# One-core attention and gated-MLP kernel: late key tiles of the last block by 256 queries, and a written-out order in place of the scheduler

## The chip, the cores and the metric

The kernel runs on one core of one Trainium2 chip. Five engines of that core take part: TensorE (matrix products, PE in the profile, its weight loads as PEld), VectorE (DVE), ScalarE (ACT), GpSimd (POOL) and SyncE (SP), which issues the transfers. The metric is device time in microseconds for one launch, the median of the runs of one kernel. A profile shows one execution and tells times from the span's start.

## What is computed

Layer norm of `x` (2048 x 512), then attention with 32 heads of 16 columns and a gated MLP of width 1792, both on the normalised input, both added to `x`:

```python
xn = _layernorm(x)
qkv = (xn @ wqkv).reshape(B, S, 3, H, Dh)            # S 2048, H 32, Dh 16
scores = einsum("bhqd,bhkd->bhqk", q, k) * Dh ** -0.5
o = einsum("bhqk,bhkd->bhqd", softmax(scores), v)
gate = xn @ W_gate;  up = xn @ W_up
return x + o.reshape(B, S, D) @ wo + (relu(gate) * up) @ W_down
```

All inputs and the output are bfloat16.

## The kernel before

**Blocks and units.** Attention runs in 32 blocks `(c4, gg, ee)`: four chunks of 512 queries, four groups of eight heads, and in each the even or the odd four heads. A block goes over 16 key tiles of 128 keys. The exponentials of one key tile (four heads by 512 queries) are made in one of two ways. As two *units*: TensorE writes scores of two heads by 512 queries into one of two pairs of PSUM banks (two operations, one on each half of the partitions), and ScalarE takes the exponential of all 128 x 1024 in one instruction into a ring of 16 buffers (L1546). Or as a *quad*: four score tiles go through one PSUM bank each to VectorE, which turns them into 16-bit integers that read as bfloat16 approximate the exponential (L1502), and two shifted patterns are added by GpSimd (L1516, for the first two and last two quads by VectorE). `QUADS` says how many of a block's 16 tiles are quads; over all blocks these are 160 of 512 tiles, and 704 units are left.

**Weighted sums.** `pv_stream` multiplies the exponentials with the values, which carry a column of ones, so that the row sum of the softmax comes along. One operation is four weight loads and four matmuls of 32 output rows each, on one half of the partitions; the halves are two operations. A unit pair gives two operations, a quad six. They accumulate over the block in one PSUM bank; in the last block the two halves have a bank each (`LAST2`). `normalise` copies the bank to SBUF, sends the row sums through two small transfers (`rsum`, `rb<-rrec`), spreads the reciprocals (L1417) and multiplies (L1420).

**The end of the kernel.** For the last block, `normalise_last` works without transfers. ScalarE copies one bank (L1291), VectorE adds the other (L1293), transposes 32 x 32 blocks so that row sums stand where they can be read (L1296), takes reciprocals (L1297), transposes them back (L1298) and multiplies (L1300); first for queries 0 to 255 of the chunk, then for 256 to 511. Each half is followed by the product with the last rows of `wo`, for two tiles of 128 output rows (`stream_out`), and the sum with the residual that was put aside earlier (`resid`, L1319); row tile 3 gets its residual from TensorE by an identity matmul (L1275) and leaves through ScalarE (L1315, L1326). The products with the two earlier head groups, four operations for each row tile, are put on TensorE behind the last weighted sums.

**Filling.** Projections, the MLP and the output rows are cut into operations that are spread over the units as `jobs`; their weights come by transfers paced to units (`paced`; W_down by `load_wd`, one tile of 14 each `D_STEP` units).

**Order.** Every operation is an `Op` with its readers and writers. `Graph.run` gives them their order: a greedy list scheduler with modelled durations, latencies and slacks (`DMA_SLACK`, `REC_SLACK`, `MUL_SLACK`), which takes the operation that can start first and, among equals, the one of least `prio`. It also chooses the buffer of each pool, and puts blank matmuls into TensorE's gaps at the start. `emit` then writes each engine's queue in that order, with a semaphore wait only where an engine has not seen the event yet. Every engine works its queue in order.

Of the kernel before, what the change touches and what calls it, by code (L numbers as in the profile page):

```python
# [12 lines left out]
ALU = mybir.AluOpType  # L13
# [22 lines left out]
D_STEP = 3.5  # L36
# [18 lines left out]
TOGETHER = 0  # L55
LAST2 = 1
LASTD = 2
TAIL_ACT = (3,)
# [14 lines left out]
QUAD_SHIFT = {(1, 3): 1, (2, 1): -1, (4, 0): -1, (6, 0): 1, (6, 3): 1, (7, 0): 1, (7, 2): 1, (8, 1): 1, (8, 4): 1, (8, 5): 1, (9, 0): 1, (9, 3): -1, (13, 1): -1, (16, 0): -1, (16, 3): 1, (18, 4): -1, (20, 2): 1, (23, 0): -1, (25, 4): -1, (26, 2): -1, (28, 0): 1, (28, 3): -1, (29, 3): 1, (30, 0): -1, (31, 1): 1}  # L73
# [14 lines left out]
QUADS = [0, 2, 5, 5, 6, 6, 4, 5, 6, 5, 5, 5, 6, 5, 5, 8, 5, 5, 4, 6, 6, 4, 6, 5, 5, 5, 5, 5, 5, 6, 5, 5]  # L88
# [44 lines left out]
class Op:  # L133
    __slots__ = ("eng", "dur", "fn", "deps", "order", "prio", "acq", "name", "idx", "start", "end",
                 "done", "left", "users", "signal", "sem", "val", "waits", "stream", "lat", "seq", "cseq", "hb", "after", "mode", "half", "bank", "urgent", "slack", "port",
                 "load", "wsrc", "wkey", "wwaits", "pair", "held")
# [9 lines left out]
class Graph:  # L146
# [5 lines left out]
    SWITCH = 107.0  # L152
    TO_POOL = 110.0
    ISSUE = 16.0
    FILL = 425.0
    NEAR = 20
    OWN = 90.0
    DMA_SLACK = 1000
    FILL_MIN = 230.0
    AHEAD_LOADS = 4  # L160
    EARLY = True
    REUSE = 5
    WIRE_LAT, WIRE_KB = 1300.0, 6.1
    WARM_AT, COLD = 7300.0, 2.0

    def __init__(self):
        self.ops = []
        self.fillers, self.nfill, self.twins = [], 0, []
        self.units = {}
# [46 lines left out]
    def run(self):  # L216
        ops = self.ops
        for o in ops:
            o.users = []
            o.held = []  # L220
        for t in {t for o in ops for t in o.acq} | {c for o in ops for t in o.acq for c in t.pool.cur if c is not None}:
            us = set(t.w + t.r)
            t.left = len(us)
            for o in us:
                o.held.append(t)
        for o in ops:
            if o.after is not None and int(o.after) > 0:
                o.order.add(self.units[min(int(o.after), len(self.units)) - 1])
            pre = set(o.deps) | o.order
            o.left = len(pre)  # L230
            for d in pre:
                d.users.append(o)
        cand = {e: [] for e in self.ENGS}
        free = {e: 0.0 for e in self.ENGS}
        self.queue = {e: [] for e in self.ENGS}
        for o in ops:
            if o.left == 0:
                cand[o.eng].append(o)
        n = 0

        def slot_for(t):

            best, second = None, None
            for i in (t.allowed if t.allowed is not None else range(len(t.pool.cur))):
                c = t.pool.cur[i]
                if c is None:
                    at = 0.0
                else:
                    at = release.get(c)
                    if at is None:  # L250
                        if c.left:
                            continue
                        at = release[c] = max(u.end for u in c.w + c.r)
                if best is None or at < best[0]:
                    best, second = (at, i), best
                elif second is None or at < second[0]:
                    second = (at, i)
            if t.pool.shared:
                held = any(c is not None and c.open > 0 for c in t.pool.cur)
                if t.extra:  # L260
                    if t.extra.slot is None:
                        return None
                elif t.open:
                    if held and not (self.EARLY and second is not None):
                        return None
                elif len(t.allowed) > 3 and (not held or any(b.slot is None and b.extra.slot is not None for b in self.twins)):
                    return second
            return best


        pe = {"mode": "full", "at": -1e9, "free": [0.0, 0.0]}
        last = {}

        known, release = {}, {}

        def bound(o):
            at = 0.0
            for d in o.deps:
                at = max(at, (self.TO_POOL if o.eng == "POOL" and d.eng not in ("POOL", "SP") else 0.0) + d.end - (self.OWN if d.eng == o.eng == "DVE" else 0.0) if d.eng == "PE" or d.eng == o.eng == "DVE" else d.end + ((0.0 if d.urgent else max(self.DMA_SLACK, o.slack)) if d.eng == "SP" else o.slack))
            for d in o.order:  # L280
                at = max(at, d.start if d.eng == o.eng else d.end)
            return at

        def ready(o):
            at = known.get(o)
            if at is None:
                at = known[o] = bound(o)
            for t in o.acq:
                if t.slot is not None:
                    continue  # L290
                b = slot_for(t)
                if b is None:
                    return None
                at = max(at, b[0] + (o.slack if o.eng == "SP" else 0.0))
            return at
# [1306 lines left out]
```

## Time and profile before

| | us |
|---|---|
| runs | 678.15, 683.24, 683.33 |
| median | 683.24 |
| profiled execution | 683.3 |
| its span | 681.3 |
| exponentials, busy (704) | 651.9 |
| ScalarE busy in all | 659.9 |
| VectorE busy | 591.3 |
| GpSimd busy | 334.6 |

The granted clock of TensorE was 1.00 in the profiled execution, 0.98 in its last 6.3 us. In the page's rows an engine's line is followed by the instruction, what it writes and reads, how often it ran, busy time, mean of one in ns, and then the engine's idle time just before it with what ended that. A row of the timeline has start, length, engine and line, and in square brackets the idle time before it. "Issue" is a wait for nothing that the profile shows. The mean of a matmul (375 ns) is its modelled length in a pipeline, not the distance of two.

### The profile page before, as it was taken

Reading aid. Unit: us, or ns where it says so; the run is one execution under the profiler, and the core shown is the slowest. Engines: PE = TensorE matmul, PEld = TensorE weight load, DVE = VectorE, ACT = ScalarE, POOL = GpSimd, SP = SyncE. Lnnn points to the kernel's source line nnn. Section 1 sums busy time; section 2 is a strip of 40 time slices with the busy share of each in tenths; the row PEclk is TensorE's granted clock in tenths of the full one; section 3 lists DMA queues with packets and bytes.
Section 4 is the critical chain, followed back from the end, with each engine's and each line's share of the span. In section 5 each row is a group of like instructions: output and inputs, shape, how many; then the busy total and the mean of one; then the engine's idle time right before and its main releaser. Section 6 shows DMA issues by size and latency. Waiting matters only on the chain.

```text
span 681.3 us, 46196 instructions
## 1 busy us (share of the span) xinstructions
PE 669.6 (98%) x22355; PEld 410.7 (60%) x20975; DVE 591.3 (87%) x1001; ACT 659.9 (97%) x721; POOL 334.6 (49%) x345
## 2 busy tenths in 40 slices
PE   8999999999999999989999999999999999999997
PEld 3456576565575765656665665556565666666664
DVE  8948999998998887989999788899989877889886
ACT  7999999999999999999999999999999999999995
POOL 3301445554455554645555564655456644435640
PEclk9999999999999999999999999999999999999999
DMA  7511011132201021110101011011200122120001
GB/s 217 79 37 28 19 39 39 40 95 67 86 12 28 24 63 36 26 47 12 45 4 36 27 49 49 24 25 28 52 6 17 32 59 60 42 52 21 23 13 34
DMA packets 51479, 28.78 MB, mean 42 GB/s; under 512 B 18840, under 2 KB 50328, under 8 KB 51288
## 3 DMA queue, kind: packets, MB, share of 16 engines
q1 hardware_dynamic: 51144, 25.70, 14.7%
q8 instruction: 169, 2.77, 1.8%
q14 instruction: 22, 0.18, 0.1%
q10 hardware_dynamic: 144, 0.13, 0.1%
HBM read 18.22 MB, written 2.10 MB: 30 GB/s over the span
## 4 chain that ended last, share of the span: by engine, by line
PE 94%; DVE 4%; DMA 1%; issue 1%; POOL 0%; DVEq 0%; SPq 0%
PE ps L141 94%; DVE qd L1502 1%; DVE stats L831 1%; DMA rb<-rrec 1%; DMA x_sb<-in_A_x_dram 0%; DVE xn_sb L854 0%; DVE mv L833 0%; DVE up_sb L1151 0%; DVE xnT L899 0%; PE ps L1275 0%; DVE qT L1086 0%; DVE xn_sb L1319 0%; DVE hT L1155 0%; DVE kT L992 0%; DVEq L605 0%
## 5 line engine op out<-in xcount | busy, mean ns | idle before, releaser
L1546 ACT ACTIVATE ring<-ps 128x1024 bf16<-128x1024 f32 x704 | 651.9, 1063 | 9.6 <-PE ps L141 8.4
L141 PE MATMUL ps<-qT,kT 64*32 64x512 bf16 x8192 | 473.6, 375 | 3.6 <-DVE qd L1502 1.8
L1516 POOL INT64_ADD qd<-qd x312 | 321.8, 1042 | 305.7 <-DVE qd L1502 189.2
L1502 DVE TENSOR_SCALAR qd<-ps 128x512 int16<-128x512 f32 x640 | 418.8, 684 | 52.1 <-PE ps L141 46.9
L141 PE MATMUL ps<-qd,v_aug 64*32 64x512 bf16 x3840 | 306.7, 375 | 0.5 <-issue 0.2
L141 PE MATMUL ps<-ring,v_aug 64*32 64x512 bf16 x2816 | 245.3, 375 | 0.8 <-issue 0.7
L1482 PEld LDWEIGHTS <-kT 64*32 64x32 bf16 x8164 | 182.2, 92 | 105.7 <-issue 26.1
L1454 PEld LDWEIGHTS <-v_aug 64*32 64x32 bf16 x5304 | 132.6, 92 | 58.9 <-issue 7.4
L141 PE MATMUL ps<-xnT,wus 64*32 64x512 bf16 x1792 | 136.4, 375 | 0.0
L141 PE MATMUL ps<-xnT,wgs 64*32 64x512 bf16 x1792 | 136.0, 375 | 0.1
L141 PE MATMUL ps<-Wd,hT 64*32 64x512 bf16 x768 | 59.5, 375 | 0.2 <-issue 0.2
L934 PEld LDWEIGHTS <-hT 64*32 64x32 bf16 x1792 | 45.8, 92 | 22.2 <-issue 3.9
L934 PEld LDWEIGHTS <-wgs 64*32 64x32 bf16 x1792 | 44.4, 92 | 22.3 <-issue 4.4
L934 PEld LDWEIGHTS <-wus 64*32 64x32 bf16 x1792 | 45.1, 92 | 19.5 <-issue 3.0
L141 PE MATMUL ps<-Wk,hT 64*32 64x512 bf16 x512 | 43.0, 375 | 0.0
L1151 DVE COPY up_sb<-ps 128x512 f32<-128x512 f32 x56 | 38.3, 684 | 5.3 <-PE ps L141 5.1
L1155 DVE SCALAR_TENSOR_TENSOR hT<-ps,up_sb 128x512 bf16<-128x512 f32 x56 | 38.2, 682 | 3.6 <-PE ps L141 3.4
L141 PE MATMUL ps<-Wv,hT 64*32 64x512 bf16 x512 | 40.3, 376 | 0.2 <-issue 0.2
L141 PE MATMUL ps<-xnT,Wq 64*32 64x512 bf16 x480 | 39.3, 375 | 0.0
L141 PE MATMUL ps<-Wo_p,x_sb 64*32 64x512 bf16 x480 | 37.8, 376 | 0.0
L141 PE MATMUL ps<-xnT,Wk 64*32 64x512 bf16 x480 | 35.7, 375 | 0.3 <-DVE xnT L899 0.3
L141 PE MATMUL ps<-Wv,xnT 64*32 64x512 bf16 x512 | 33.0, 375 | 0.4 <-issue 0.2
(83 smaller groups left out, 221.9 us busy)
## 6 DMA issues: line engine op xcount, KB each, us to landing
wus<-in_B_W_up_dram SPq DMA_DIRECT2D x38, 128.0 KB, 2.6
wgs<-in_B_W_gate_dram SPq DMA_DIRECT2D x38, 128.0 KB, 3.0
xr_sb<-in_A_x_dram SPq DMA_DIRECT2D x16, 128.0 KB, 2.3
qT<-qf SPq DMA_DIRECT2D x120, 16.0 KB, 2.5
o_sb<-o_sb SPq DMA_DIRECT2D x60, 32.0 KB, 2.5
out_dram<-xn_sb SPq DMA_DIRECT2D x15, 128.0 KB, 1.8
x_sb<-in_A_x_dram SPq DMA_DIRECT2D x8, 128.0 KB, 2.8
Wd<-in_B_W_down_dram SPq DMA_DIRECT2D x6, 128.0 KB, 2.3
```

The source lines that it names most:

```text
L141: return e.add_instruction(mybir.InstMatmult(name=e.bass.get_next_instruction_name(), engine=mybir.EngineType.PE, ins=[e.lower_ap(x), e.lo ...
L831: G.op("DVE", 580, lambda e, m=m: e.bn_stats(stats[:, m, :], xs(m)), reads=[t_xm[m]], writes=[t_st], prio=pr, order=last_xn if m == 4 and ...
L934: e.ldweights(w()[rows, 32 * j:32 * j + 32], tile_position=(rows.start, 32 * j))
L1151: G.op("DVE", 603, lambda e: e.tensor_copy(up_sb[:, tup.slot, :], bank_of(tu)), reads=[tu], writes=[tup], prio=-590)
L1155: G.op("DVE", 603, lambda e: e.scalar_tensor_tensor(out=hT[:, th.slot, :], in0=bank_of(tg), scalar=0.0, in1=up_sb[:, tup.slot, :], op0=ALU ...
L1454: e.ldweights(vs(j), tile_position=(64 * half, 32 * j))
L1482: e.ldweights(ks(m), tile_position=(64 * half, 32 * m))
L1502: G.op("DVE", 601, lambda e, j=j, tx=tx: e.tensor_scalar(qd[:, tq.slot, 512 * j:512 * j + 512], ps[:, BANK[tx.slot], :], IBIAS[3], 0.0, op ...
L1516: G.op("POOL", POOL_NS, lambda e, x=x, n=n: e.int64_add(x().bitcast(I64), raw().bitcast(I64), SHIFTS[n + 1] * LANES), reads=[ti, tq, t_lib ...
L1546: exp_ops[u] = G.op("ACT", ACT_NS, lambda e, tr=tr, k0=k0: e.activation(ring[:, tr.slot, :, :], ps[:, 4 * k0:4 * k0 + 2, :], ACTF.Exp, sca ...
```

## The change

In the last block, key tiles from `QCUT` = 10 on are *parted*: a unit then holds four heads by 256 queries instead of two heads by 512, and the units are sorted so that all of queries 0 to 255 come first, then all of 256 to 511. The quads of that block are moved into its first ten tiles. The block has three accumulators: one for tiles 0 to 9, copied to SBUF when they are done, and one of 256 columns for each half of the queries. The first half's closing takes its sums as soon as the first six parted units are in, with the priority `EARLY_PRIO`; the first addend now comes from SBUF, and ScalarE's copies are gone.

```diff
-LAST2 = 1
+EARLY_PRIO = -700
+QCUT = 10
+LAST_PV = 4
...
-D_STEP = 3.5
+D_STEP = 3.25
...
+        def parted(key):
+            return key[:3] == blocks[-1] and key[3] >= QCUT
...
+                if bk == blocks[-1]:
+                    dve_kt[bk] = [QCUT * t // NT for t in dve_kt[bk]]
...
-        units = [k + (p,) for k in keys for p in range(2) if k not in kinds]
+        units = [k + (p,) for k in keys for p in range(2) if k not in kinds and not parted(k)]
+        units += [k + (p,) for p in range(2) for k in keys if k not in kinds and parted(k)]
...
+            def sc_q(e):
+                ins = None
+                for v in range(2):
+                    for m in range(4):
+                        ins = matmul_loaded(e, ps[32 * m:32 * m + 32, bank(), 256 * v:256 * v + 256], ks(m), qT[rows, tq.slot, 2 * v + ee, 256 * p:256 * p + 256], True, True, (64 * half, 32 * m))
+                return ins
...
-            if p:
+            if split:
+                pv_stream(key[:3], key[3], [(lambda rows, j=j, tr=tr: ring[rows, tr.slot, j // 2, 256 * (j % 2):256 * (j % 2) + 256]) for j in range(4)], [tr], u, u + PV_LAG, qh=p)
+            elif p:
```

In the closing, for half `h` of the queries, VectorE's first step changes, and the products with the earlier head groups for row tiles 0 and 1 may start before the last weighted sums (in `before`, two operations for each group):

```diff
-                G.op("ACT", 300, lambda e, c=c: e.activation(up_sb[:, tup.slot, c], at_bank(tp)[:, c], ACTF.Copy), reads=[tp],
-                     writes=[th] if h else [tup, th], joins=[tup] if h else [], prio=-950 + h)
-                G.op("DVE", 340, lambda e, c=c: e.tensor_tensor(o_sb[:, tos.slot, c], up_sb[:, tup.slot, c], at_bank(tp_hi)[:, c], ALU.add),
+                tp = tps[h]
+                G.op("DVE", 380, lambda e, c=c, tp=tp: e.tensor_tensor(o_sb[:, tos.slot, c], at_bank(tp)[:, 0:256], o_sb[:, tos.slot, c], ALU.add), reads=[tp, tos], writes=[to], prio=-950 if h else EARLY_PRIO, order=half_done)
...
                 for i in (2 * h, 2 * h + 1):
+                    if not h:
+                        before(i, [prev_d])
```

`Graph.run` and its model are removed. `ORDER`, a list of 8048 numbers, names each operation by the number under which it was made, all engines in one sequence; seven entries of -1 are blank matmuls. `SLOTS` gives the buffers in the order in which they are taken. `follow` walks the list and fills the engines' queues; `emit` writes waits as before. In `QUADS` block 29 has seven quads instead of six and block 31, the last, four instead of five. `QUAD_SHIFT` is changed at some thirty places too, so quads of many blocks stand one or two tiles elsewhere.

```diff
+    def follow(self, order, slots):
         self.queue = {e: [] for e in self.ENGS}
+        last, port, slots = {}, None, iter(slots)
+        for i in order:
+            if i < 0:
+                o = Op()
...
+            else:
+                o = self.ops[i]
+            e = o.eng
             for t in o.acq:
                 if t.slot is not None:
                     continue
...
+                t.slot = next(slots)
...
-        G.run()
+        G.follow(ORDER, SLOTS)
```

The end of the list; ahead of these lines come `7956, 7876, 7989, 8012, 7951, 7981, 7936, 8007, 7994, 8013, 7976, 7991, 7986, 8020, 8014`:

```diff
+    8008, 7990, 8021, 8009, 7985, 7975, 7995, 8015, 8022, 7996, 8010, 8011, 7998, 8003, 8023, 8028, 7999, 8016, 8004, 8024, 8029, 8017, 8000, 8030, 8005,
+    8025, 8031, 8032, 8018, 8001, 8006, 8002, 8019, 8026, 8033, 8037, 8034, 8027, 8038, 8035, 8039, 8036, 8040,
```

403 lines of the change are left out of this document (106 added, 297 removed), and 313 rows, old and new, of the table ORDER.

## The prediction

> **What bounds the kernel now.** I read the page's head and its engine rows first, then ScalarE's own timeline, then what it waited for, then the last ten microseconds instruction by instruction, and last the chain of waits.
>
> ```profile
> span 681.3 us, 46196 instructions
> PE 669.6 (98%) x22355; PEld 410.7 (60%) x20975; DVE 591.3 (87%) x1001; ACT 659.9 (97%) x721; POOL 334.6 (49%) x345
> PE 94%; DVE 4%; DMA 1%; issue 1%; POOL 0%; DVEq 0%; SPq 0%
> L1546 ACT ACTIVATE ring<-ps 128x1024 bf16<-128x1024 f32 x704 | 651.9, 1063 | 9.6 <-PE ps L141 8.4
> ```
>
> Two engines look full. TensorE's 98% busy and its 94% of the chain say little, since its ends are modelled and it nearly always has something; ScalarE's 704 exponentials, one per unit, fill 651.9 us of the 681.3, so the kernel is a queue of exponentials with a head, a few gaps and a tail.
>
> ```profile
> 10.32 1.96 ACT L1546 ACTIVATE ring<-ps 128x1024 bf16<-128x1024 f32 x2
> 12.44 1.02 ACT L1546 ACTIVATE ring<-ps 128x1024 bf16<-128x1024 f32 x1 [0.17 <-PE ps L141]
> 13.92 4.73 ACT L1546 ACTIVATE ring<-ps 128x1024 bf16<-128x1024 f32 x5 [0.46 <-PE ps L141]
> 19.21 12.95 ACT L1546 ACTIVATE ring<-ps 128x1024 bf16<-128x1024 f32 x14 [0.55 <-PE ps L141]
> ...
> 169.17 56.54 ACT L1546 ACTIVATE ring<-ps 128x1024 bf16<-128x1024 f32 x61 [1.27 <-PE ps L141]
> ...
> 264.17 11.46 ACT L1546 ACTIVATE ring<-ps 128x1024 bf16<-128x1024 f32 x12 [0.54 <-PE ps L141]
> ...
> 294.11 122.16 ACT L1546 ACTIVATE ring<-ps 128x1024 bf16<-128x1024 f32 x132 [1.61 <-PE ps L141]
> ...
> 663.35 8.41 ACT L1546 ACTIVATE ring<-ps 128x1024 bf16<-128x1024 f32 x9
> ```
> ```profile
> ACT ring L1546 <- PE ps L141: 8.4, 20, 1.6
> ```
>
> Exponentials run from 10.32 to 663.35 + 8.41 = 671.76. The 132 of the longest stretch take 122.16 us, 0.925 us each; 704 of them would take 651.5, and the 661.4 us between first and last hold 9.9 more. 8.4 of these are 20 waits for TensorE's scores. After the last exponential 681.3 - 671.76 = 9.5 us remain. So there are three terms: 651.5 us of exponentials, which stay (the diff adds a key tile to the exponentials of one block and takes one from another, and its quad counts still sum to 160), about 10 us of gaps and 9.5 us of tail. The profiled execution took 683.3 us, 2.0 around its span; the runs were 678.15, 683.24 and 683.33, so it stands at their median.
>
> ```profile
> 672.24 0.66 ACT L1291 ACTIVATE up_sb<-ps 128x256 f32<-128x256 f32 x2 [0.47 <-PE ps L141]
> 672.74 0.41 DVE L1293 TENSOR_TENSOR o_sb<-up_sb,ps 128x256 f32<-128x256 f32 x1
> ...
> 674.39 0.43 DVE L1300 TENSOR_TENSOR qf<-o_sb,up_sb 128x256 bf16<-128x256 f32 x1
> 674.61 1.13 PE L1275 MATMUL ps<-xnT,identf 128*128 128x512 f32 x2
> 674.73 0.41 DVE L1293 TENSOR_TENSOR o_sb<-up_sb,ps 128x256 f32<-128x256 f32 x1
> ...
> 676.37 0.42 DVE L1300 TENSOR_TENSOR qf<-o_sb,up_sb 128x256 bf16<-128x256 f32 x1
> 676.72 1.88 DVE L1319 TENSOR_TENSOR xn_sb<-ps,xnT 128x512 bf16<-128x512 f32 x3
> ...
> 676.86 1.04 PE L141 MATMUL ps<-Wo_l,qf 64*32 64x512 bf16 x16 [0.15 <-DVE qf L1300]
> ...
> 677.95 0.60 ACT L1315 ACTIVATE xn_sb<-ps 128x512 bf16<-128x512 f32 x1 [5.04 <-PE ps L141]
> ```
>
> The tail is serial. Weighted sums are finished at 672.24. VectorE then closes the first 256 queries (672.74 to 674.82, 2.1 us: add, transpose, reciprocal, transpose, multiply), and only after that the other 256 (674.73 to 676.79). Then come the projection, four row tiles and the stores, 681.3 - 676.79 = 4.5 us.
>
> **The change, part by part.** These rows price its operations:
>
> ```profile
> 660.00:670.00 10.00, 10.00 (x372) 6.71 (x322) 8.10 (x15) 10.00 (x12) 1.17 (x2) 1.00 0.04 7
> 668.11 0.38 PE L141 MATMUL ps<-qd,v_aug 64*32 64x512 bf16 x4
> 668.54 0.38 PE L141 MATMUL ps<-ring,v_aug 64*32 64x512 bf16 x4
> 668.75 0.38 PE L141 MATMUL ps<-ring,v_aug 64*32 64x512 bf16 x4
> L141 PE MATMUL ps<-qd,v_aug 64*32 64x512 bf16 x3840 | 306.7, 375 | 0.5 <-issue 0.2
> L1364 DVE COPY o_sb<-ps 128x512 f32<-128x512 f32 x31 | 21.1, 681 | 4.3 <-PE ps L141 4.3
> ```
>
> From 668.54 to 668.75 an operation (four matmuls of 512 columns, one for each 32 output rows) takes 0.215 us on its half of the partitions; the two halves work side by side, so one leaves each 0.108 us.
>
> *The tail.* Late units hold four heads by 256 queries, and those of queries 0 to 255 come first. Their closing needs nothing from the last six units, so it can run under them. When it really runs is in the order: the list is one sequence over all engines, and the last 43 operation numbers are those of the closing. Counting back from the last one, 8040, the first half's five VectorE steps are 8007 to 8011, the second half's 8028 to 8032; the twelve late units are five operations each, 7937 to 7996, so the last weighted sums are 7996 and those of the first half end with 7951. On TensorE's queue 7951 is followed by 14 operations and then 7996: 15 x 0.108 = 1.6 us. Taking 672.3 for the end of 7996, the first half's sums are there at 670.7. Right ahead of 8007 on VectorE stands one new step, 7936, the copy that empties the accumulator of tiles 0 to 9, 0.68 us by the row of its like (L1364); if it ran only then, 8007 would start at 671.4. I take 671.0. The first half then closes until 673.1, and the second starts at 673.1 instead of 674.73: 1.6 us less. Bounds: 672.24, if VectorE is free when the sums end (2.5 less), and 671.76 + 2.08 = 673.84, if the first half starts only with the last exponential's end (0.9 less). Behind 8007 only closing steps stand on VectorE, so its wait for the sums holds up nobody else.
>
> Against it stands one queue. The identity matmul that adds the residual for row 3 (8002) ended at 674.61 + 1.13 = 675.74, one microsecond before the second multiply, hidden. In the new list it is directly ahead of the last projection, behind nine operations of which the first waits for the first half's multiply. Four operations of the last projection took 1.04 us, 0.26 each, since their halves wait for each other; nine take 1.0 us at 0.108 and 2.3 at 0.26. So it ends between 673.1 + 1.0 + 1.13 = 675.2 and 676.5, and the second multiply at 673.1 + 2.06 = 675.2: between nothing and 1.3 us of it come out. The nine are for three rows whose halves can alternate; I take 0.4. The tail's sum is -1.6 + 0.4 = -1.2 us. VectorE still writes rows 0, 1 and 2 after the second multiply (8018, 8026, 8035), as now, so the 4.5 us stay. ScalarE's two copies go; they lie in the 674.73 - 671.76 = 2.97 us already counted.
>
> *The narrow matmuls.* Twelve units each issue two score operations of eight 256-column matmuls instead of four of 512, and two weighted-sum operations per unit instead of per two units: 24 instructions per unit become 40, 192 more in all. No 256-column matmul of this tile is in the trace. By columns the added cost is nil; by instructions (372 + 322 in 10.00 us, 14.4 ns each) it is 192 x 14.4 = 2.8 us. I take nil, nearest to the row at 668.11: four matmuls together last 0.38 us, no longer than the single one's 375 ns in the page's groups, so they start together. And the quads, which stood up to tile 13 and now end at tile 7, take some of TensorE's load out of the last 11 us. The Trainium skill ("TensorE: Matmul & The Clock Gate", section "Wait — 56ns, not 53.3ns?") says that matmuls never start less than about 25 ns apart, however narrow; the row at 668.11 speaks against that for four tiles that lie beside each other. By that rule 12 x 24 narrow matmuls would take 7.2 us instead of 3.9 by columns, and the sum below would be up to 3.3 us longer, 683.1.
>
> *The body.* All other edits act through the order: W_down's loads move a quarter unit closer together per tile, quads shift, the last two blocks trade one. W_down and the quads have rows:
>
> ```profile
> L783 SPq DMA_DIRECT2D Wv<-in_B_W_down_dram x4: 327/342/377, 165.2 to 180.8; - x4
> L141 PE MATMUL ps<-Wd,hT x768: 372/376/382, 213.4 to 667.0; 64*32 64x512 bf16 x192
> 600.00:625.00 25.00, 24.87 (x856) 16.05 (x800) 23.54 (x40) 24.84 (x28) 11.36 (x11) 1.00 0.18 45
> L1502 DVE TENSOR_SCALAR qd<-ps 128x512 int16<-128x512 f32 x640 | 418.8, 684 | 52.1 <-PE ps L141 46.9
> ```
>
> The last load is issued at 180.8, the first use is at 213.4: nothing. Block 29's seventh quad costs VectorE four more evictions in a stretch where it is busy 23.54 of 25 us (600 to 625); but block 15 has eight already and lies inside the 122 us without a wait, so I cost it at zero, at most 4 x 0.684 = 2.7 us.
>
> What remains is where the gaps fall. Two kinds are visible:
>
> ```profile
> 262.48 0.38 PE L141 MATMUL ps<-ring,v_aug 64*32 64x512 bf16 x3
> 263.33 0.37 PE L141 MATMUL ps<-ring,v_aug 64*32 64x512 bf16 x1 [0.47 <-issue]
> ...
> 292.09 0.01 DVE L1417 LOAD_MASK_SELECT rb<-rb  x1 [2.01 <-DMA rb<-rrec]
> q8 instruction: 169, 2.77, 1.8%
> L1417 DVE STREAM_SHUFFLE rb<-rb 128x512 f32<-128x512 f32 x16 | 11.8, 736 | 0.0
> DVE rb L1417 <- DMA rb<-rrec: 3.1, 3, 2.0
> ```
>
> At 262.48 a group of four breaks off after three; inside a group no semaphore is waited for, so the fourth instruction itself was late, which fits the 169 packets of 16 KB on the instruction queue. ScalarE paid 0.54 us. At 292.09 VectorE stood with scores queued behind it for a transfer, and ScalarE paid 1.61. Both depend on what the order puts beside what. The Trainium skill ("Runtime: NRT & Kernel Launch", Instruction fetch mechanics) calls crossing a 16 KiB block mostly hidden; here it is not always. By that page the order could change nothing in gaps of the first kind.
>
> A new order rolls these gaps anew. Bounds: 8.4 us less (all of them gone) and 8.4 more (twice as many). Nearest to the rows is that the two longest, 1.61 and 1.27, which each need a coincidence of place, do not return and 0.3 us each of common size takes their place: -2.3 us. Forecast: 683.3 - 1.2 - 2.3 = 679.8 us, 0.5% faster, inside the 1% (6.8 us) that a measurement of this kernel can tell from no change. Its own range is 677 to 682.5.
>
> **The rivals.** *Most gaps go.* The list is no longer the outcome of a greedy rule; if it puts transfers away from the points where instructions run short, all waits but the prologue's (0.17, 0.46 and 0.55, together 1.2) vanish. For it: the gaps are few, 20, and each has a local cause; the change's own note says that program blocks are in the order. Against: the list shows no margin, and nothing in the diff touches the instruction queue. 683.3 - 1.2 - 7.2 = 674.9; 671 to 676.4.
>
> *TensorE too dense at the end.* If narrow matmuls cost by instruction, 2.8 us, scores of the last units come late, and the tail's gain is eaten: 683.3 - 1.2 + 2.8 = 684.9 with the gaps as they are, 682.6 with the gaps' forecast. For it: 660 to 670 is full. Against: ScalarE ran nine exponentials there without a gap. The skill's rule on 25 ns, above, is of this kind and points the same way.
>
> *Slower: the wait at the spread.* The reciprocals' transfer is waited for by VectorE in its fixed place (L1417), and behind it stand the evictions that free PSUM for scores. The old scheduler kept explicit slack there (REC_SLACK, DMA_SLACK); the new code follows a list without any. Of the 16 spreads three waited, together 3.1 us, and one cost ScalarE 1.61. Five more like that one, 8.1 us, would make it slower by 1%; six more give 683.3 - 1.2 + 9.7 = 691.8. Against: slack can be in the list all the same, and 13 of 16 spreads did not wait.
>
> *Nothing but the tail.* 683.3 - 1.2 = 682.1; a tail that gains nothing, with the same gaps, gives 683.3.
>
> **How the numbers follow.** Forecast 0.37, tail alone 0.12, dense end 0.11, most gaps gone 0.30, waits at the spread 0.10. The forecast, the tail alone and the dense end lie within 1%: 0.60; faster 0.30, slower 0.10. The range takes the fast case down to 671 and the dense end and one or two spread waits up to 685.5.
>
> **What would show it.** Right: exponentials as many, 704; a gap from the last exponential to the second half's add near 1.3 us instead of 2.97, with the identity matmul just ahead of the last projection; ScalarE's waits for scores near 6 us; no wait of VectorE over 1 us for the reciprocals. Wrong: scores of the last twelve units late (a ScalarE wait after 660), a first half that closes only after the last exponential, or ScalarE's waits over 10 us.

## The result and the profile after

| | before | after |
|---|---|---|
| median of six runs, us | 682.18 (678.15 to 683.33) | 704.43 (703.22 to 705.60) |
| profiled execution, its span | 683.3, 681.3 | 704.59, 702.2 |
| first exponential starts, last ends | 10.32, 671.76 | 10.53, 694.19 |
| from the last exponential to the end | 9.5 | 8.0 |

The change makes the kernel slower: ratio 1.0334, 95% interval 1.0304 to 1.0363. The forecast was 679.8 with a range up to 685.5; it was wrong, and in its sign.

First the head, the chain and ScalarE's group from the page of the profile after (same order as before; TensorE's matmuls now carry L483 and the exponentials L1677):

```profile
span 702.2 us, 46398 instructions
PE 689.3 (98%) x22499; PEld 384.0 (55%) x21027; DVE 598.7 (85%) x1002; ACT 670.5 (95%) x719; POOL 333.8 (48%) x345
q8 instruction: 170, 2.79, 1.7%
PE 90%; ACT 3%; DVE 3%; DMA 2%; SPq 1%; issue 1%; POOL 0%; DVEq 0%
L1677 ACT ACTIVATE ring<-ps 128x1024 bf16<-128x1024 f32 x704 | 663.3, 1035 | 20.4 <-PE ps L483 15.1
```

Still 704 exponentials. They are shorter one by one (1035 ns, before 1063), and yet together they reach 22.2 us further: 683.7 us from the first to the last instead of 661.4. Some of the 43 stretches of ScalarE's timeline:

```profile
10.53 1.96 ACT L1677 ACTIVATE ring<-ps 128x1024 bf16<-128x1024 f32 x2
...
218.91 72.97 ACT L1677 ACTIVATE ring<-ps 128x1024 bf16<-128x1024 f32 x77 [0.22 <-PE ps L483]
...
569.50 67.90 ACT L1677 ACTIVATE ring<-ps 128x1024 bf16<-128x1024 f32 x71 [0.16 <-PE ps L483]
...
666.72 21.18 ACT L1677 ACTIVATE ring<-ps 128x1024 bf16<-128x1024 f32 x22 [1.16 <-PE ps L483]
688.11 2.85 ACT L1677 ACTIVATE ring<-ps 128x1024 bf16<-128x1024 f32 x3 [0.21 <-PE ps L483]
691.34 2.85 ACT L1677 ACTIVATE ring<-ps 128x1024 bf16<-128x1024 f32 x3 [0.38 <-PE ps L483]
```

The timeline begins a new stretch only at a wait of 0.15 us or more. Of those there are 42 instead of 20, 15.1 us instead of 8.4: 6.7 us more. The group's row holds the shorter waits too: its idle time is 20.4 us, before 9.6, by the trace's records in 130 places, before 43. That is 10.8 us more.

The rest is overlap that is lost. Exponentials that don't wait follow each other most often at 0.904 us, in both traces, though each lasts 1.04 to 1.06 us: they overlap. One that waits starts after the end of the one ahead, which costs 0.13 us besides the idle time shown. 87 more waits cost 87 x 0.13 = 11.3 us, and 10.8 + 11.3 = 22.1. Exponentials without a wait are no slower than before, 0.921 us apart on average against 0.918.

In the longest stretch 77 exponentials take 72.97 us; without the last one's own length (1.02), that is 71.95 / 76 = 0.947 us from start to start, short waits included. Before, in the stretch of 132, it was (122.16 - 1.02) / 131 = 0.925. It is no single accident: counted along the timeline, the kernel is behind by 3.7 us at unit 300, 11.9 at unit 500 and 22.4 at the end.

The list of waits, with total, times and longest in us, shows whom TensorE keeps waiting, and what its own weight loads show (L1611 scores, L1050 projections, L1581 weighted sums):

```profile
DVE qd L1637 <- PE ps L483: 62.7, 156, 1.3
PEld L1611 <- issue: 31.5, 115, 0.8
PEld L1050 <- issue: 28.3, 109, 1.3
PEld L1581 <- issue: 19.3, 81, 0.6
ACT ring L1677 <- PE ps L483: 15.1, 42, 1.2
```

The same rows before (L1502, L1482, L934, L1454):

```profile
DVE qd L1502 <- PE ps L141: 46.9, 97, 1.1
PEld L1482 <- issue: 26.1, 84, 2.1
...
PEld L934 <- issue: 18.8, 60, 1.0
...
PEld L1454 <- issue: 7.4, 31, 0.5
```

VectorE waits for scores 156 times instead of 97 (62.7 us, before 46.9), ScalarE 42 times instead of 20, and weight loads stand 79 us instead of 52 with nothing to wait for in the profile. Both consumers wait more for the same producer, TensorE. As TensorE in turn waits for banks that they empty, this alone doesn't tell where the time starts. VectorE's waits for the reciprocals' transfer (3.1 us before) are gone: the list has none.

The tail, from VectorE's rows of the timeline after 693 us, with the identity matmul and the last projection:

```profile
693.38 0.42 DVE L1419 TENSOR_TENSOR o_sb<-ps,o_sb 128x256 f32<-128x256 f32 x1 [0.36 <-PE ps L483]
...
695.04 0.42 DVE L1426 TENSOR_TENSOR qf<-o_sb,up_sb 128x256 bf16<-128x256 f32 x1
...
695.38 0.42 DVE L1419 TENSOR_TENSOR o_sb<-ps,o_sb 128x256 f32<-128x256 f32 x1
...
697.00 1.12 PE L1402 MATMUL ps<-xnT,identf 128*128 128x512 f32 x2
697.03 0.42 DVE L1426 TENSOR_TENSOR qf<-o_sb,up_sb 128x256 bf16<-128x256 f32 x1
...
698.07 1.04 PE L483 MATMUL ps<-Wo_l,qf 64*32 64x512 bf16 x16
```

The first half of the queries closes under the last exponentials: its add starts at 693.38, 0.8 us before they end at 694.19. The second add follows them by 695.38 - 694.19 = 1.2 us (2.97 before). The tail is 702.2 - 694.19 = 8.0 us.

### The profile page after: what moved, and what is told of

The parts are those of the page before. It is cut to its first block, busy times and chain, and to the rows that moved or that the text cites. A ratio compares the mean times of both kernels' runs of the same rounds, so it can differ in the third digit from the quotient of the medians.

```text
span 702.2 us, 46398 instructions
## 1 busy us (share of the span) xinstructions
PE 689.3 (98%) x22499; PEld 384.0 (55%) x21027; DVE 598.7 (85%) x1002; ACT 670.5 (95%) x719; POOL 333.8 (48%) x345
## 4 chain that ended last, share of the span: by engine, by line
PE 90%; ACT 3%; DVE 3%; DMA 2%; SPq 1%; issue 1%; POOL 0%; DVEq 0%
PE ps L483 90%; ACT ring L1677 3%; DVE qd L1637 1%; SPq L977 1%; DMA xnT<-xn_sb 1%; DMA xr_sb<-in_A_x_dram 1%; DVE stats L947 0%; DMA x_sb<-in_A_x_dram 0%; DVE xn_sb L970 0%; SPq L1260 0%; SPq L860 0%; DVE xnT L1015 0%; SPq L1317 0%; PE ps L1402 0%; ACT up_sb L939 0%
## 5 line engine op out<-in xcount | busy, mean ns | idle before, releaser
L1677 ACT ACTIVATE ring<-ps 128x1024 bf16<-128x1024 f32 x704 | 663.3, 1035 | 20.4 <-PE ps L483 15.1
L1637 DVE TENSOR_SCALAR qd<-ps 128x512 int16<-128x512 f32 x640 | 421.5, 686 | 69.0 <-PE ps L483 62.7
L483 PE MATMUL ps<-qT,kT 64*32 64x512 bf16 x8288 | 476.4, 372 | 3.5 <-ACT ring L1677 1.2
L483 PE MATMUL ps<-qd,v_aug 64*32 64x512 bf16 x3840 | 299.2, 375 | 0.4
L483 PE MATMUL ps<-ring,v_aug 64*32 64x512 bf16 (+1 forms) x2864 | 241.3, 371 | 0.3 <-ACT ring L1677 0.3
L1611 PEld LDWEIGHTS <-kT 64*32 64x32 bf16 x8156 | 172.8, 92 | 119.5 <-issue 31.5
L1581 PEld LDWEIGHTS <-v_aug 64*32 64x32 bf16 x5364 | 128.9, 92 | 73.5 <-issue 19.3
L483 PE MATMUL ps<-xnT,wgs 64*32 64x512 bf16 x1792 | 135.0, 374 | 0.6
L483 PE MATMUL ps<-xnT,wus 64*32 64x512 bf16 x1792 | 132.8, 375 | 0.9 <-DVE qd L1637 0.8
L483 PE MATMUL ps<-Wd,hT 64*32 64x512 bf16 x768 | 60.9, 375 | 0.1
L1050 PEld LDWEIGHTS <-wgs 64*32 64x32 bf16 x1792 | 43.8, 92 | 29.0 <-issue 6.7
L1050 PEld LDWEIGHTS <-wus 64*32 64x32 bf16 x1792 | 43.8, 92 | 27.5 <-issue 7.8
L1050 PEld LDWEIGHTS <-hT 64*32 64x32 bf16 x1792 | 43.6, 92 | 23.3 <-issue 3.8
L483 PE MATMUL ps<-Wk,hT 64*32 64x512 bf16 x512 | 44.4, 375 | 0.0
L483 PE MATMUL ps<-Wv,hT 64*32 64x512 bf16 x512 | 42.5, 375 | 0.0
L1277 DVE SCALAR_TENSOR_TENSOR hT<-ps,up_sb 128x512 bf16<-128x512 f32 x56 | 38.4, 685 | 3.6 <-PE ps L483 2.8
L483 PE MATMUL ps<-Wo_p,x_sb 64*32 64x512 bf16 x480 | 39.4, 375 | 0.1
L483 PE MATMUL ps<-xnT,Wq 64*32 64x512 bf16 x480 | 38.1, 375 | 0.0
L483 PE MATMUL ps<-xnT,Wk 64*32 64x512 bf16 x480 | 36.6, 375 | 1.0 <-DMA xnT<-xn_sb 0.7
L483 PE MATMUL ps<-Wv,xnT 64*32 64x512 bf16 x512 | 32.6, 374 | 0.5 <-DVE qd L1637 0.4
```

The lines of the kernel that those rows point to most:

```text
L483: return e.add_instruction(mybir.InstMatmult(name=e.bass.get_next_instruction_name(), engine=mybir.EngineType.PE, ins=[e.lower_ap(x), e.lo ...
L1050: e.ldweights(w()[rows, 32 * j:32 * j + 32], tile_position=(rows.start, 32 * j))
L1277: G.op("DVE", 603, lambda e: e.scalar_tensor_tensor(out=hT[:, th.slot, :], in0=bank_of(tg), scalar=0.0, in1=up_sb[:, tup.slot, :], op0=ALU ...
L1581: e.ldweights(vs(j), tile_position=(64 * half, 32 * j))
L1611: e.ldweights(ks(m), tile_position=(64 * half, 32 * m))
L1637: G.op("DVE", 601, lambda e, j=j, tx=tx: e.tensor_scalar(qd[:, tq.slot, 512 * j:512 * j + 512], ps[:, BANK[tx.slot], :], IBIAS[3], 0.0, op ...
```

## The experiments

A *score operation* is the one that writes scores (`ps<-qT,kT`); a TensorE operation works on half 0 or half 1 of the partitions. Two counts of each program are used, from TensorE's queue as it is written: neighbours of one half (640 of 5559 before, 2114 of 5571 after), and *close waits*, operations that wait for the end of one of the other half in the same bank standing at most four places ahead (187 before, 245 after). Medians are in us, ratios to the kernel before on the same chip; it took 680.2 to 682.9 us on the chips used, so runs are compared with each other by their ratios. In diffs of `ORDER` a number is an operation.

### The layout or the list?

*greedy_layout*: parted key tiles, quads and closing as in the change, but ordered by the old scheduler.

```diff
-        G.follow(ORDER, SLOTS)
+        G.fillers = [(P_b, 0, "pvz", blank_early, "full")]
+        G.run()
```

> The changed kernel's last block, quads and constants, but its order made by the old scheduler instead of the list. Theory of the halves: the layout is innocent and brings its tail, 679 to 683 us (682.2 less 1.2). Rival of the layout: near 704. Rival of the waits: as the halves, 679 to 685, since the order is the old scheduler's.

Measured: 682.40 against 682.91, ratio 0.9999 [0.9973, 1.0026]. The whole loss is the list's: ScalarE's own order is the same in both kernels, that of the other four engines differs. From its page, list of waits and ScalarE's timeline:

```profile
span 679.3 us, 46386 instructions
ACT ring L1561 <- PE ps L141: 6.2, 13, 0.8
```
```profile
19.21 145.80 ACT L1561 ACTIVATE ring<-ps 128x1024 bf16<-128x1024 f32 x158 [0.56 <-PE ps L141]
...
664.81 3.99 ACT L1561 ACTIVATE ring<-ps 128x1024 bf16<-128x1024 f32 x4 [0.30 <-PE ps L141]
```

(145.80 - 1.02) / 157 = 0.922 us from exponential to exponential, 13 waits, and the last one ends at 668.80, 3.0 earlier than before. But its tail is 679.3 - 668.80 = 10.5 us: with the old order the closing by halves is no gain.

### TensorE's queue or the other engines'?

Two mixed orders. *list_but_tensor* takes ScalarE's, VectorE's, GpSimd's and SyncE's order and the buffers from the list and lets the old scheduler order TensorE; *tensor_of_list* takes TensorE's queue from the list and leaves the rest to the scheduler. In the scheduler's choice:

```diff
             for o in cand["PE"]:
+                if "PE" in FIXED and o is not line["PE"][head["PE"]]:
+                    continue
                 at = ready(o)
```

> The changed kernel: ScalarE, VectorE, GpSimd, SyncE and all buffers follow the list; TensorE's queue alone is made by the old scheduler's rule. Same-half neighbours 902 (list 2114, old scheduler 648). Theory of the halves, and any theory that puts the loss into TensorE's queue: 680 to 689 us. Rival (the other engines' order or the buffers): 697 to 706.

> The reverse: TensorE's queue is the list's, same-half neighbours 2114; the other engines' order and the buffers are made by the old scheduler around it. Theory of the halves: 697 to 710 us. Rival (the other engines' order): 680 to 689.

Measured: 698.53, ratio 1.0255 [1.0191, 1.0319], and 709.24, ratio 1.0418 [1.0357, 1.0478], where the list itself gives 1.0334. TensorE's queue of the list is enough for the whole loss, with the other engines' order made around it. But the list's other orders and buffers lose 18 us too, with a TensorE queue made around them: there the rival's forecast came true and not that of the halves. The two shares don't add up, and these two runs don't clear the other engines' order.

### Halves side by side

*alternated* and *alternated_half* sort TensorE's operations anew, in all of the list or in its first 4024 entries: where two neighbours share a half, one of the other half is pulled ahead from up to eight places behind.

```diff
-        G.follow(ORDER, SLOTS)
+        G.follow(*G.alternate(ORDER, SLOTS, 8, lambda last, half, n: half == last))
```

> The changed kernel; only TensorE's queue is re-sorted: where two neighbouring operations use the same half of the partitions, the next operation of the other half (among the next eight, and only if all it needs stands earlier in the list) is pulled ahead. Same-half neighbours fall from 2114 to 48 of 5571 (the kernel before has 640). Theory of the halves (a half stands idle while TensorE's queue is stuck behind an operation of the other half): most of the 22 us return, 682 to 689 us. Rival of the waits (the list puts operations where their semaphores come late, on whichever half): stays within 3 us of 704. Rival of the layout (256-column units, moved quads): stays at 704.

> The changed kernel re-sorted as in the first run, but only in the first half of the list; same-half neighbours 1110. Theory of the halves: half of the loss returns, 690 to 697 us, and ScalarE's exponentials keep a short pitch up to the middle and a long one after it. Rivals: 704.

Measured: 862.91, ratio 1.2659 [1.2626, 1.2692], and 780.70, ratio 1.1454 [1.1418, 1.1490], with only 48 neighbours of one half left in the first. The sorting had a side effect that the counts of its program show: operations on the two halves of one accumulator now follow each other directly, and 496 operations wait for the end of the one just ahead, 2 in the change. In all fifteen traces that were laid out along the program's order, such an operation starts 0.44 us or more after the one of 512 columns that it waits for; two neighbours start 0.108 apart otherwise. 494 x (0.44 - 0.108) = 164 us, against 862.9 - 704.4 = 158.5 measured. The run measures close waits, not halves.

*before_runs* writes the order of the kernel before as a list and takes the alternation out: at every fifth place the next operation of the same half is pulled ahead, from up to six places behind, which makes 2186 neighbours of one half. *before_swaps* exchanges 995 pairs of one half two places apart in it, which keeps 640:

```diff
-    3747, 4137, 3749, 4279, 4121, 4092, 4138, 4296, 4297, 4123, 4094, 4216, 4096, 4298, 3750, 4224, 4139, 4301
+    3745, 4121, 3749, 4279, 4137, 4092, 4138, 4296, 4297, 4216, 4094, 4123, 4139, 4298, 3750, 4224, 4096, 4301
```

> The kernel before, its own order as a list, with TensorE's queue alone re-sorted the other way: at every fifth place the next operation of the same half is pulled ahead of one of the other half. Same-half neighbours rise from 640 to 2186 (the changed kernel: 2114). Theory of the halves: loses what the change lost, 697 to 708 us. Rival of the waits: little, 682 to 687, since operations move by at most six places. Rival of the layout: 682 to 685.

> The kernel before as a list, with 995 pairs of TensorE's operations that stand two places apart, on the same half, exchanged: as many operations move as in the run with added runs (884 ahead there, by 1.4 places; 995 here, by 2), but which half stands at which place is not changed at all (640 same-half neighbours). Theory of the halves: 682 to 690 us. Rival of the waits (an operation out of its time is what costs): 700 to 720, like the run with added runs (712.8).

Measured: 712.75, ratio 1.0461 [1.0430, 1.0492], and 730.45, ratio 1.0729 [1.0656, 1.0803]. The second lost more without a single neighbour more, and more than either theory forecast, so the first proves nothing of halves. Both also have more close waits than the 187 of their base, 283 and 305 (54 of the latter directly behind, 3 before), so neither is a clean measure of anything but exchanges of all kinds together.

*neighbours_swapped* is the gentle form: 585 direct neighbours of the list change places, 0 0 1 1 becoming 0 1 0 1. Neighbours of one half fall to 944, an operation moves by one place, and close waits stay about as many (237).

```diff
-    4213, 3667, 3671, 4214, 4070, 3669, 4033, 4029, 4218, 4069
+    4213, 3667, 4214, 3671, 4070, 3669, 4033, 4029, 4218, 4069
```

> The changed kernel's list with 585 pairs of direct neighbours on TensorE exchanged, where two of one half are followed by two of the other (0 0 1 1 becomes 0 1 0 1): every operation moves by one place at most, same-half neighbours fall from 2114 to 944. Theory of the halves: 684 to 694 us. Rival of the waits: 702 to 715, no better than the list or worse.

Measured: 693.52, ratio 1.0181 [1.0122, 1.0241], where the list has 1.0334: about 10 of the 22 us are back, by the two intervals 6 to 15. Its ScalarE stretches:

```profile
99.33 70.84 ACT L1719 ACTIVATE ring<-ps 128x1024 bf16<-128x1024 f32 x76
...
550.52 75.66 ACT L1719 ACTIVATE ring<-ps 128x1024 bf16<-128x1024 f32 x81 [0.42 <-PE ps L525]
```

(70.84 - 1.02) / 75 = 0.931 us from start to start, against 0.947 in the change. Laying the matmul records along the program's order tells what a half of TensorE stood idle for. A half is idle from 0.216 us after the start of its last operation (0.11 after a narrow one) to the start of the next; the figures are the mean of the two halves, from the first exponential to the last. As the matmuls are as many, the total only tells the kernel's time over again; the parts say more.

| idle time of a half, us | before | after | *neighbours_swapped* |
|---|---|---|---|
| all | 65.0 | 86.5 | 74.1 |
| ahead of an operation that itself waits for another engine or a transfer | 38.4 | 48.8 | 43.2 |
| ahead of one that itself waits for an operation of TensorE | 10.2 | 15.3 | 13.3 |
| ahead of one that waits for nothing, behind one of the other half | 12.8 | 21.2 | 16.2 |
| other | 3.6 | 1.2 | 1.4 |

That operations of one half in a row let the other half run dry fits the fourth row: it grew by 8.4 us, and 5.0 of them came back when the halves alternate. But it is less than half of the 21.5 added; 10.4 stand ahead of operations that wait for another engine.

### What is the other half of the loss?

Four ideas were tried by exchanges of a few hundred to a thousand pairs of TensorE operations, one to three places apart (up to six in *others_exchanged*), starting from the list and from the scheduler's order for the new layout (that of 682.40).

*Close waits.* *waits_apart* moves them apart in the list (245 to 74 in the program), *both_mended* also mends halves (57, and 1116 neighbours), *greedy_mended* does it in the scheduler's order (187 to 52).

```diff
-    4298, 3750, 4302, 4092, 4124, 4122, 4157, 4095, 4320, 4140
+    4298, 3750, 4092, 4302, 4124, 4122, 4157, 4320, 4095, 4140
```

> The list with 458 exchanges of TensorE operations one to three places apart, chosen so that an operation that must wait for the end of one of the other half in its bank stands five or more places behind it: such pairs at one to four places fall from 245 to 76, neighbours of one half rise from 2114 to 2300. Theory of two costs: by the idle time that the traces show for such a wait (0.45, 0.3, 0.11 and 0.06 us at one to four places) 18 us of it go and the new neighbours bring 2 back, so 704 - 16 = 688; if half of that idle time is covered, 697. Rival (the remainder lies in the other engines' order, and in displacement): 704 or more.

> The list with 974 such exchanges, chosen for both: waits at one to four places from 245 to 57 and neighbours of one half from 2114 to 1116. Theory of two costs: 704 - 17 - 9 = 678; with half of the waits' idle time covered 686. It should lie below the 693.5 of the swapped neighbours by 7 to 16 us. Rival (other engines' order holds the other 11 us): 693 or more.

> The old scheduler's order for the new layout with 383 such exchanges: waits at one to four places from 187 to 52, neighbours of one half from 648 to 720. Theory of two costs: 682.4 - 11.4 + 0.7 = 672, or 677 with half of the idle time covered: faster than both kernels. Rival (the old scheduler's order has no such time to give, since its waits lie beside ScalarE's): 682 to 690.

Measured: 707.72, ratio 1.0408 [1.0373, 1.0442]; 703.98, ratio 1.0359 [1.0320, 1.0398]; 690.28, ratio 1.0151 [1.0121, 1.0181]. No gain from fewer close waits, and in *both_mended* even the gain of the alternation is gone again, though it has nearly as few neighbours of one half. There the idle time ahead of operations that wait for one of TensorE did fall, from 15.3 to 10.8 us, but that ahead of operations that wait for another engine rose from 48.8 to 52.8. Close waits are not the rest.

*Any displacement.* *order_exchanged* exchanges 497 pairs two places apart in the scheduler's order, with halves and close waits as they were.

```diff
-    4426, 4381, 4633, 4634, 4428, 4383, 4465, 4481, 4533, 4635, 4430, 4541, 4482, 4638
+    4633, 4381, 4426, 4634, 4481, 4383, 4465, 4428, 4533, 4635, 4638, 4541, 4482, 4430
```

> The layout of the change with the order that the old scheduler makes for it (682.4 us), in which 497 pairs of TensorE operations of one half, two places apart, change places. Alternation stays (648 neighbours of one half), and so does the distance between an operation and the operation of the other half whose end in the same bank it waits for. Theory of two costs in the list (neighbours of one half, and waits for the other half's end from fewer than five places behind): 682, within 3 us. Rival (any displaced operation costs, as the 995 exchanges that gave 730 seemed to say, 0.048 us each): about 706.

Measured: 697.14, ratio 1.0250 [1.0216, 1.0285]. The theory of two costs falls: against 0.9999 for the scheduler's order that is 17 us lost, 0.034 for each exchange, less than the rival's 0.048.

*Scores that come too early.* 439 of these exchanges had moved a score operation ahead, and the traces put much of the added idle time of the change ahead of score operations (49 us on a half; 34 before, for which the expectations below take 31). So *others_exchanged* leaves scores in place and exchanges 410 pairs of others, and three runs move the score operations that stood idle back by one or two places: *scores_later* in the list, *swapped_scores_later* in that of the swapped neighbours, *greedy_scores_later* in the scheduler's order.

```diff
-    4179, 3660, 4024, 3985, 3983, 4181, 3593, 4180
+    4179, 3660, 3985, 3983, 4024, 4181, 3593, 4180
```

> The old scheduler's order for the new layout (682.4 us) with 410 exchanges of TensorE operations one to six places apart, none of them a score operation; neighbours of one half 654 instead of 648, waits for the other half's end at one to four places 198 instead of 187. In the 497 exchanges that gave 697.1, 439 moved a score operation two places ahead. Theory (what costs is a score operation that comes ahead of the release of its bank, so that TensorE stops for ScalarE or VectorE): 682 to 686. Rival (any displaced operation costs 0.03 us, as there): 682 + 410 x 0.03 = 694 or more.

> The list with the score operations of 243 units and quads moved one or two places back on TensorE, those that the trace of the change shows standing idle (on ScalarE's or VectorE's release, or behind such a one); nothing else is chosen, neighbours of one half 2214 instead of 2114, close waits unchanged. Idle time ahead of score operations was 49 us on a half there and 31 us in the kernel before. Theory (scores stand too early in the list): 690 to 697. Rival (the engines that release the banks are late themselves, so that a later score only makes ScalarE wait): 704 or more.

> The list with the 585 swapped neighbours (693.5 us), and the score operations of 242 units and quads that stood idle in its trace moved one or two places back. Theory: the two add up, 680 to 687, so that nothing of the 22 us is left for the other engines' order. Rival: 693 or more.

> The old scheduler's order for the new layout (682.4 us) with the score operations of 116 units and quads that stood idle in its trace moved one or two places back. Theory: its scores stand about right, idle time ahead of them is 31 us and half of it could go: 676 to 682, which would beat both kernels. Rival (each was placed at the first moment at which it could start, and a later place makes ScalarE or VectorE wait): 683 to 690.

Measured: 698.24, ratio 1.0227 [1.0188, 1.0266]; 713.85, ratio 1.0452 [1.0414, 1.0490]; 702.82, ratio 1.0293 [1.0256, 1.0330]; 691.54, ratio 1.0118 [1.0075, 1.0162]. All lose against their base, with and without scores among the moved; *greedy_scores_later* came out above both of its forecasts. In *scores_later* ScalarE simply waits longer, as the rival said:

```profile
L1719 ACT ACTIVATE ring<-ps 128x1024 bf16<-128x1024 f32 x704 | 665.8, 1033 | 27.6 <-PE ps L525 23.2
```

*A misfit of the other engines.* *others_exchanged_matched* keeps TensorE's queue of *others_exchanged* and lets the scheduler make VectorE's and SyncE's order and the buffers for it (the edit is that of *tensor_of_list*).

> TensorE's queue of the run with 410 exchanges of operations other than scores (698.2 us), operation by operation, while the old scheduler makes the order of VectorE and SyncE and chooses the buffers for it (85 of VectorE's 986 places differ from the order of the 682.4 us kernel; ScalarE's and GpSimd's order stay). Theory of a misfit (exchanges cost because the other engines' fixed orders no longer fit the arrival of TensorE's results): 682 to 688. Rival (TensorE's queue itself loses the time, since its operations come to their turn before their inputs are there): 695 or more.

Measured: 703.63, ratio 1.0336 [1.0293, 1.0380]. The scheduler moved 85 places of VectorE and 8 of SyncE and gave nothing back, so a misfit that its modelled durations can mend is not it.

### The closing alone

*greedy_list_closing*: the scheduler's order, with the last 150 operations over all engines in the list's order.

```diff
-    7910, 7855, 7962, 7963, 7918, 7857, 7837, 7859, 7940
+    7846, 7855, 7859, 7853, 7926, 7934, 7927, 7919, 7866
```

> The old scheduler's order for the new layout (682.4 us), of which the last 150 operations over all engines stand in the list's order instead. The tail after the last exponential was 10.5 us with the old scheduler's order and 8.0 with the list's. If the list's closing does by itself what it did behind the list, 682.4 - 2.5 = 679.9, a bit faster than both kernels. Rival (the exchanged operations delay the last units' scores as elsewhere, some 40 TensorE operations by 0.03 us and more): 682 to 685.

Measured: 682.34, ratio 1.0029 [1.0006, 1.0051]. Its timeline:

```profile
core 0 of [0], span 680.3 us
...
664.35 4.69 ACT L1719 ACTIVATE ring<-ps 128x1024 bf16<-128x1024 f32 x5 [3.49 <-PE ps L525]
669.48 2.85 ACT L1719 ACTIVATE ring<-ps 128x1024 bf16<-128x1024 f32 x3 [0.44 <-PE ps L525]
```

The last exponential ends at 672.33 and the tail is 680.3 - 672.33 = 8.0 us, 2.5 less than with the scheduler's closing. At the seam ScalarE waits 3.49 us, which eats it. No kernel of this study is faster than the one before.

## Why the prediction was wrong

**The first term.** "651.5 us of exponentials, which stay" took 0.925 us for ScalarE's own pace. It holds waiting too: where nothing is waited for, the distance is most often 0.904, and 704 x 0.904 = 636.4. Measured as the prediction did it, on the longest stretch, the term is 704 x 0.947 = 666.7 after, 15 us more where nothing was to change. Its row could have warned: instructions of 1063 ns at a distance of 925 overlap, so each wait also costs overlap, and the row's idle time, 9.6, stood beside 8.4 of listed waits. The chain of waits, 94% TensorE, was read and set aside with "say little"; it named the engine that both consumers then waited for.

**The body.** "A new order rolls these gaps anew", within 8.4 us less or more, was the step that failed. The listed waits did stay within it (15.1 us, 6.7 more), beyond the 10 us that the prediction named as a sign of being wrong; with the short waits and the lost overlap they cost 22. And the gaps weren't the known ones rolled anew, since both kinds that the prediction priced went away. Breaks of over 0.3 us inside a group of four were 15 before (7.6 us) and are 2 after (0.8). VectorE's waits for the reciprocals' transfer, 3.1 us before, are gone. What grew in their place was put at nothing: the order of TensorE's queue was treated as luck at a few places, when it acts on nearly every unit.

*greedy_layout* shows that the layout is innocent, *tensor_of_list* that the list's queue of TensorE is enough for the loss. *neighbours_swapped* got about half of it back by letting the halves alternate; *both_mended*, with 1116 neighbours of one half, got nothing back, so their count alone doesn't set the time. What exactly costs the rest stays open: close waits, early scores and a misfit of the other engines were tried and are not it. What the runs do show is that the scheduler's order for the new layout lost from each of four sets of exchanges, by the ratios between 0.03 us (383 exchanges, 10 us) and 0.07 (116 moves of scores, 8 us) for each. The list lost 0.01 to 0.03 from two sets (458 and 243), nothing clear of the noise from 974, and gained from 585. The scheduler took the operation that can start first, and that order has hardly any room; that the list was made for other durations than the chip's would explain it, but is only argued.

**The tail.** Right. Forecast -1.2 us, measured 8.0 - 9.5 = -1.5. The first half's add was forecast 0.76 us before the last exponential's end (671.0 against 671.76) and came 0.8 before; the second add was forecast 1.3 after it and came 1.2. The identity matmul did come out, by 698.12 - 697.45 = 0.7 us, inside the range of nothing to 1.3, where 0.4 was taken. From the second multiply's end to the end it is 702.2 - 697.45 = 4.75 us instead of 4.5, so about 0.2 of it lengthened the tail.

**The narrow matmuls.** Right, they cost nothing. After, in the timeline of TensorE:

```profile
690.45 0.27 PE L483 MATMUL ps<-qT,kT 64*32 64x256 bf16 x4 [0.22 <-issue]
690.46 0.27 PE L483 MATMUL ps<-ring,v_aug 64*32 64x256 bf16 x4
690.56 0.27 PE L483 MATMUL ps<-qT,kT 64*32 64x256 bf16 x4
690.57 0.27 PE L483 MATMUL ps<-ring,v_aug 64*32 64x256 bf16 x4
...
690.68 0.38 PE L483 MATMUL ps<-qT,kT 64*32 64x256 bf16 x8
```

From 690.45 to 690.68 the two halves start sixteen narrow matmuls in 0.23 us, 14 ns each; a group of four takes 0.11 us on its half, half of the wide one's 0.215. The Trainium skill ("TensorE: Matmul & The Clock Gate", section "Wait — 56ns, not 53.3ns?") has no matmuls start less than about 25 ns apart, however narrow. For tiles side by side this trace doesn't agree: with 14 ns on average, the measurement decides. ScalarE's two waits after 688 us, 0.6 together, leave nothing of the 2.8 us of a dense end either.

**The rivals.** The one that ended slower had the wrong mechanism: no wait of VectorE for the reciprocals' transfer is left. Its remark that the new code follows a list without any slack was nearer than its place. *Most gaps go* was right that late instructions and transfers would hold up less, and wrong that ScalarE's waits would vanish with them. Late instructions are no part of the loss: the instruction queue moved 170 packets, before 169, and their breaks became fewer. So the order does change gaps of the first kind, unlike what the prediction says.

## What to carry to other kernels

When instructions of an engine overlap, compare their distance from start to start, and not the listed waits alone: here a wait showed 0.16 us of idle time on average (20.4 us in 130 places) and cost 0.13 more in lost overlap. An order that keeps two engines near full is a part of the kernel like any other, and replacing it is the largest edit of a change, however small the others look. Its counts (neighbours of one half, waits on the operation just ahead) show that it differs before anything is run, though they didn't foretell the time here. When a change brings a new layout and a new order at once, run the new layout under the old scheduler first.

## What the runs showed of the hardware

TensorE doesn't start matmuls strictly in the order of its queue when they lie on different halves, unlike what the description of the kernel says. Laid along the program's order, 826 of the 5572 operations of the change started over 0.1 us ahead of at least one earlier operation of the other half (92 before): 654 passed one, 150 two, 22 three, none more. At 108.33 us, for instance, a weighted sum of half 0 started 0.15 and 0.37 us ahead of two projections of half 1 that stand before it. No operation passed more than three, and the list has 114 rows of four to six operations of one half (18 before).

An operation that waits for the end of one of the other half in its bank starts at the least 0.44 us after that one's start, in all fifteen traces that were laid out, and 0.33 us where the awaited one is of 256 columns. One place behind, such a half stood idle for 0.51 us (496 operations of *alternated*), three places behind for 0.11, four for 0.07 and five for 0.03 (84, 141 and 164 operations of the change).

TensorE does run out of instructions. Inside a group of four no semaphore is waited for, and each of the 17 breaks of over 0.3 us there, 15 before and 2 after, ends 1.25 to 1.6 us after a packet of 16 KB ended on the instruction queue. Only 11% of all these matmuls start at that distance from a packet's end.
